# Routed attention and gated MLP on one core: four stages of three units a pair, one rotation of PSUM bank pairs, a bound moved to GpSimd

## The chip, the cores and the metric

The kernel runs on one core of a Trainium2 chip. The metric is the device time of one execution in microseconds (us). The engines are named as in the profile: PE is TensorE (its weight loads are listed as PEld), DVE is VectorE, ACT is ScalarE, POOL is GpSimd, SP is SyncE, which here only issues DMAs.

## The reference: what is computed

Four batches of eight heads, 768 tokens, head size 64. Every query and every key is assigned to the one of 16 centroids of its head that it is most similar to. A query attends only to the keys of its own cluster: softmax of `q k / 8` over these, times `v`. The result, read as 3072 tokens by 512, goes through an MLP:

```python
q_assign = argmax(normalize(q) @ normalize(c).T); k_assign = argmax(normalize(k) @ normalize(c).T)
scores = where(q_assign[:, None] == k_assign[None, :], q @ k.T / sqrt(64), -1e9)
attn = exp(scores - rowmax(scores)); attn /= attn.sum(-1) + 1e-9
x = attn @ v                              # then (B, S, H * D) as 3072 x 512
h = x @ w_in                              # 512 x 2048
out = (h * erf(softplus(h))) @ w_out      # 2048 x 512
```

All inputs and outputs are float32.

## The kernel before

**Work and units.** Heads are taken two at a time: a *pair* p (0 to 15), with head e=0 on partitions 0 to 63 and e=1 on 64 to 127. A pair's scores are computed transposed, in 12 *units*: two halves of 384 queries, and in each half six tiles j of 128 keys. One unit is a PSUM tile of 128 keys by 2 heads by 384 queries, which takes two PSUM banks. A core has eight banks. Two are the tiles `turned[0]` and `turned[1]`; the other six are the subject of this case.

**What a unit needs.** `products(u)` multiplies float32 k by q into the unit's two banks `sc`. `scores(u)` adds a bfloat16 matmul of `km` and `qm` on top: one-hot cluster vectors times a huge number, and one row that holds the query's shift (minus its maximum). `curve(u)` is ACT's exponential from PSUM into one of eight tiles `pr`. Later `accumulate(u)` adds `pr` on POOL (the softmax denominator; five additions per half, of which the first adds two tiles of `pr`), and `attend(u)` multiplies by v on PE into `turned[half]`. After the sixth unit of a half, `divide` sums the accumulated tile over partitions on PE into the other `turned` bank (the rows `turned<-more_out,minus`), takes Ln and Exp on ACT (`inv`), and in two further steps three DVE instructions (`den`, `turned`, `more_out`), then a DMA of the result to DRAM.

**Maxima, a pair ahead.** The shift of pair p+1 needs its row maxima. `maxima_step(p, i)`, 12 per pair, recomputes the masked scores in bfloat16 with queries on partitions (four matmuls into the two banks `wide`), and DVE reduces them from PSUM (`nmx`). After steps 5 and 11 a small DVE reduction (`lowest`) completes a half, and `turn` transposes the result on PE into `turned[half]`, from which ACT copies two rows into `qm`. The step runs six units ahead of the unit it stands beside. `masks` makes `qm` and `km` of pair p+1: a matmul with `pick` into a `turned` bank and an ACT copy out of it, four per pair. `similarities` and `choose` make the assignment of pair p+2 (one matmul group, four DVE instructions), `transposes` (two DVE instructions) and `vectors` (two ACT casts) its operands.

**Weight conversions.** In the background, weights are brought from DRAM as 512 KB pieces into five places and split into a form that later matmuls use: `size_and_rest` (two ACT instructions), `bounded` (DVE maximum with 2.0), `sign` (ACT), `shifted` (DVE shift by 3 bits), `summed` (POOL addition, which then frees the place and issues the next fetch on SP). 22 of the 32 pieces (`N_EARLY`) are done during the attention, two per pair. `FORMS` says in which periods the later pairs do sums of converted weights on DVE.

**The order of the work.** The order is written out by hand and kept: every engine executes its instructions in the order in which the program issues them, and waits where an operand or a buffer isn't ready. Before, a pair is six *periods* of two units (`period(p, i)`). A period issues, on PE: a `turn` if one is due (periods 0 and 3), a maxima step, the products of two units, a second maxima step, the scores of both, in period 3 the similarities, and then the `attend` of the two units of the period before, in periods 0 and 3 also the sum for `divide`. Masks stand in periods 0, 2 and 5. Tile mode matters on PE: products, scores, maxima and masks use 64 rows by 128 columns, so two matmuls (one per head) run side by side in the two row halves; `attend`, `turn` and the sum use 128 rows by 64 columns. In the profile these are marked `64*128` and `128*64`.

PSUM before: the maxima have their own two banks, `wide`, used by every step in turn; the units rotate through two pairs of banks (`ps_s`, two buffers).

After the attention comes the MLP, with the rest of the conversions; nothing in its order is touched.

## Time and profile before

| | us |
|---|---|
| median of three runs | 1022.67 (1022.65 to 1023.0) |
| the profiled execution's own time | 1022.77 |
| its span in the profile | 1021.1 |
| attention, steady: one pair (191.30 to 217.70) | 26.4 |
| first matmul of the MLP (`bank<-x_own,w_in`) | at 436.6 |

The span is what the trace covers, from the first to the last instruction; some 1.7 us of the execution lie around it. Busy times of PE overlap: a matmul's record runs until its result is out, while the next one has begun, so two consecutive *starts* tell more of PE's pace than durations do. In a row of the timeline the first number is the start, the second the time until the last of the merged instructions ends, and a bracket tells how long the engine was idle before and what released it. The granted clock was 1.00 in the whole attention.

### The profile page before, as it was taken

How to read it: one execution, taken by the hardware profiler on the slowest of the kernel's cores; microseconds unless marked ns; L12 is line 12 of the kernel's file. 1: busy time of each engine (PE TensorE's matmuls, PEld its weight loads, DVE VectorE, ACT ScalarE, POOL GpSimd, SP SyncE). 2: the span in 40 equal slices, each digit the busy share in tenths (PEclk: the TensorE clock that was granted, in tenths of full speed). 3: DMA queues.
4: the chain of work that ended last, by engine and by line, in shares of the span. 5: the costliest groups of instructions: out<-in, count | busy, mean ns of one | idle time of the engine just before them, and what ended most of it. 6: DMA issues, size and time to landing. Idle time of an engine off the chain costs nothing.

```text
span 1021.1 us, 15464 instructions
## 1 busy us (share of the span) xinstructions
PE 1013.9 (99%) x5930; PEld 726.1 (71%) x5930; DVE 695.8 (68%) x1305; ACT 515.0 (50%) x673; POOL 345.7 (34%) x229
## 2 busy tenths in 40 slices
PE   8999999999999999999999999999999999999998
PEld 3555555554555445478888888888888888888887
DVE  8777777777777777778875674756565547565754
ACT  3787877787777666567615142322233141505050
POOL 1777777777777667745130000000000000000000
PEclk9999999999999999999999999999999999999999
DMA  9344444444343311041100100110011000000001
GB/s 214 68 98 97 104 104 103 104 104 104 83 104 87 76 28 32 24 154 61 42 1 21 63 1 1 42 42 1 1 41 42 1 21 22 1 1 21 21 1 41
DMA packets 141641, 55.55 MB, mean 54 GB/s; under 512 B 127104, under 2 KB 131456, under 8 KB 141568
## 3 DMA queue, kind: packets, MB, share of 16 engines
q1 hardware_dynamic: 139216, 54.28, 20.8%
q8 instruction: 46, 0.75, 0.3%
q10 hardware_dynamic: 2352, 0.30, 0.2%
q14 instruction: 27, 0.22, 0.1%
HBM read 41.98 MB, written 12.58 MB: 53 GB/s over the span
## 4 chain that ended last, share of the span: by engine, by line
PE 97%; DVE 1%; POOL 0%; ACT 0%; issue 0%; DVEq 0%; ACTq 0%; POOLq 0%
PE bank L63 43%; PE turned L63 33%; PE sc L63 15%; PE wide L63 7%; DVE nmx L63 1%; POOL more_out L63 0%; DVE sims L63 0%; ACT inv L63 0%; DVE kT L63 0%; DVE qT L63 0%; ACT pr L63 0%; DVE hotT L63 0%; DVE wide L63 0%; DVE den L63 0%; DVE hot L63 0%
## 5 line engine op out<-in xcount | busy, mean ns | idle before, releaser
L63 POOL TENSOR_TENSOR more_out<-more_out,pr 128x768 f32<-128x768 f32 x128 | 223.5, 1746 | 67.6 <-ACT pr L63 62.5
L63 DVE TENSOR_REDUCE nmx<-wide 128x2 f32<-128x768 f32 x189 | 180.7, 956 | 95.1 <-PE wide L63 70.8
L63 ACT ACTIVATE pr<-sc 128x768 f32<-128x768 f32 x192 | 147.0, 810 | 75.0 <-PE sc L63 75.0
L63 PE MATMUL turned<-pr,in_v 128*64 128x386 f32 x768 | 145.5, 500 | 0.1
L63 DVE TENSOR_TENSOR g<-bank,g 128x256 f32<-128x256 f32 x222 | 89.5, 421 | 52.9 <-PE bank L63 46.3
L63 PE MATMUL bank<-x_own,w_in 128*128 128x256 f32 x424 | 104.5, 380 | 0.0
L63 PE MATMUL bank<-w_out,g 128*128 128x256 f32 x448 | 103.1, 379 | 0.0
L63 PE MATMUL sc<-qT,kT 64*128 64x384 f32 x528 | 99.7, 484 | 0.0
L63 PEld LDWEIGHTS turned<-pr,in_v 128*64 128x64 f32 x768 | 46.7, 136 | 72.2 <-issue 71.1
L63 PEld LDWEIGHTS bank<-w_out,g 128*128 128x128 f32 x448 | 85.2, 190 | 11.5
L63 PEld LDWEIGHTS bank<-x_own,w_in 128*128 128x128 f32 x424 | 80.4, 190 | 12.1 <-issue 1.2
L63 ACT COPY g<-bank 128x256 f32<-128x256 f32 x28 | 10.4, 372 | 152.5 <-PE bank L63 148.5
L63 DVE TENSOR_TENSOR osb<-bank,osb 128x256 f32<-128x256 f32 x87 | 35.4, 420 | 72.8 <-ACT osb L63 25.4
L63 ACT ACT_TABLE_LOAD x48 | 61.6, 1283 | 45.7 <-DVE g L63 45.0
L63 POOL TENSOR_TENSOR more_out<-pr,pr 128x768 f32<-128x768 f32 x32 | 58.8, 1837 | 58.5 <-ACT pr L63 58.5
L63 PE MATMUL bank<-x_more,more_in 128*128 128x256 f32 x296 | 76.0, 379 | 0.0
L63 PEld LDWEIGHTS <-qv 64*128 64x128 bf16 x384 | 25.6, 93 | 65.2 <-issue 51.1
L63 PE MATMUL wide<-kv,qv 64*128 64x384 bf16 x378 | 69.4, 328 | 1.1 <-ACT km L63 0.6
L63 PEld LDWEIGHTS sc<-qT,kT 64*128 64x128 f32 x528 | 56.6, 187 | 16.6 <-issue 1.2
L63 PE MATMUL wide<-km,qm 64*128 64x384 bf16 x378 | 68.3, 322 | 0.0
L63 PE MATMUL bank<-more_out,g_more 128*128 128x256 f32 x272 | 64.3, 379 | 0.0
L63 DVE TENSOR_TENSOR g<-a_s,g 128x512 f32<-128x512 f32 x96 | 62.4, 688 | 1.4 <-ACT a_s L63 1.4
(162 smaller groups left out, 1710.2 us busy)
## 6 DMA issues: line engine op xcount, KB each, us to landing
x_own<-in_moe_w_in_dram SPq DMA_DIRECT2D x13, 512.0 KB, 4.3
in_v<-in_v_dram SPq DMA_DIRECT2D x32, 192.0 KB, 2.9
x_dram<-more_out SPq DMA_DIRECT2D x32, 192.0 KB, 2.4
x_own<-x_dram SPq DMA_DIRECT2D x6, 1024.0 KB, 5.1
out_dram<-osb SPq DMA_DIRECT2D x23, 256.0 KB, 2.0
in_k<-in_k_dram SPq DMA_DIRECT2D x59, 96.0 KB, 2.7
in_q<-in_q_dram SPq DMA_DIRECT2D x58, 96.0 KB, 3.6
g_more<-in_moe_w_out_dram SPq DMA_DIRECT2D x6, 512.0 KB, 3.6
```

The lines of the kernel that those rows point to most:

```text
L63: ins = getattr(self.engine, name)(*args, **kw)
```

## The change

1. A pair is four *stages* of three units (`three(p, i)`) in place of six periods of two. A stage issues, per unit, one maxima step (`ahead`: seven units ahead in the steady state), the products, the scores and the exponential of that unit; then the `attend` of the three units of the stage before. `divide` begins at the end of stages 0 and 2, its DVE steps come in the next stage, all three between the second and the third maximum.
2. `wide` is gone. Maxima and units rotate through one pool of three pairs of banks (`two_banks`), in the order in which they are issued: maximum, unit, maximum, unit. So a tile takes the banks of the tile issued three places before it. `choose` takes its little maximum from the same rotation.
3. `turn` moves from the start of a period to the place between the second and the third unit's `attend`, in stages 1 and 3.
4. The masks stand at stage 0 (three of them) and stage 2 (one).
5. Three conversions in two pairs instead of four; all 22 are still done before the attention ends. `bounded` is issued on POOL for these, after the additions; `shifted` stands in stage 0 of each pair and in stage 2 of odd pairs, after the third maximum's reduction (and, in stage 0, ahead of the two `transposes`, which are now both there). `size_and_rest` is split in two.
6. `FORMS`, the places' order, the two `load_x` and the opening follow from that.

```diff
-    11: {5: 1}, 12: {0: 1, 2: 1, 5: 1}, 13: {0: 1, 2: 1, 5: 1}, 14: {0: 2, 2: 1, 3: 1, 5: 1},
-    15: {0: 1, 2: 1, 3: 2, 4: 2, 5: 2},
+    8: {2: 1}, 10: {2: 1}, 12: {0: 1, 2: 1}, 14: {0: 2, 2: 2, 3: 1}, 15: {0: 2, 1: 1, 2: 4, 3: 4},
...
-MASKS = {(0, 1): ("k", 0), (0, 2): ("k", 1), (2, 0): ("q", 0), (5, 0): ("q", 1)}
-FIRST_MASKS = {(2, 0): ("k", 0), (2, 1): ("q", 0), (2, 2): ("k", 1), (5, 0): ("q", 1)}
+MASKS = {(0, 0): ("k", 0), (0, 1): ("q", 0), (0, 2): ("k", 1), (2, 0): ("q", 1)}
+FIRST_MASKS = {(1, 1): ("k", 0), (1, 2): ("q", 0), (2, 0): ("k", 1), (2, 2): ("q", 1)}
...
-    ps_s = passing("ps_s", 2, space=PSUM)
-    wide = passing("ps_w", 1, space=PSUM).tile([P, 2, 512], F32, name="wide")
+    ps_s = passing("ps_s", 3, space=PSUM)
+
+    def two_banks():
+        return ps_s.tile([P, 2, 512], F32, name="sc", tag="s")
...
-    def bounded(n):
+    def bounded(n, engine=ve):
         w = w_steps[n][0]
-        ve.tensor_scalar(out=w, in0=w, scalar1=2.0, scalar2=None, op0=ALU.max)
+        engine.tensor_scalar(out=w, in0=w, scalar1=2.0, scalar2=None, op0=ALU.max)
...
-        mx = (wide[:, 0] if spare is None else spare)[:, 512 - n :]
+        mx = (two_banks()[:, 0] if spare is None else spare)[:, 512 - n :]
...
-    def maxima_step(p, i, sm=wide):
+    def maxima_step(p, i):
...
+        sm = two_banks()
...
-        sc = sc_of[u] = ps_s.tile([P, 2, 512], F32, name="sc", tag="s")
+        sc = sc_of[u] = two_banks()
...
-    def step_ahead(u):
-        p, i = divmod(u + NJ, 2 * NJ)
-        if p < NPAIR:
-            maxima_step(p, i)
+    ahead = [[u + NJ + 1] for u in range(len(units) - NJ - 1)] + [[] for _ in range(NJ + 1)]
+    ahead[0:NJ] = [[], [], [7, 8], [9], [10], [11]]
+    for u in range(NJ, 2 * NJ):
+        ahead[u] = [u + NJ]
+    ahead[2 * NJ - 1].append(3 * NJ)
...
+    def conversions(p, i):
+        a = 3 * (p // 2)
+        of = {
+            (0, 0): [(shifted, a - 1), (sign, a - 1)],
+            (0, 1): [(size, a)],
+            (0, 2): [(rest_of, a)],
+            (0, 3): [(size, a + 1)],
+            (1, 0): [(shifted, a), (sign, a)],
+            (1, 1): [(rest_of, a + 1)],
+            (1, 2): [(shifted, a + 1), (sign, a + 1), (size, a + 2)],
+            (1, 3): [(rest_of, a + 2)],
+        }[p % 2, i]
+        for f, n in of:
+            if 0 <= n < N_EARLY:
+                f(n)
+    def sums(p, i):
+        a = 3 * (p // 2)
+        of = {
+            (0, 1): [(summed, a - 1)], (0, 2): [(bounded, a)], (1, 0): [(bounded, a + 1)],
+            (1, 1): [(summed, a)], (1, 3): [(summed, a + 1), (bounded, a + 2)],
+        }.get((p % 2, i), [])
+        for f, n in of:
+            if 0 <= n < N_EARLY:
+                f(n, *([ge] if f is bounded else []))
+                if f is summed and n == N_EARLY - 4:
+                    load_x(0)
+                elif f is summed and n == N_EARLY - 1:
+                    load_x(1)
+    def three(p, i):
+        u = 2 * NJ * p + 3 * i
 
         def mask(place):
             which = (MASKS if p else FIRST_MASKS).get((i, place))
             if which:
-                return masks(p + 1, *which, turned[0 if i in (0, 5) else 1])
+                return masks(p + 1, *which, turned[0 if p and i == 0 else 1])
             return lambda: None
-        if u > 0:
-            for which in turns if i in (0, 3) else ():
-                turn(*which)
-                turns.remove(which)
-            step_ahead(u)
-        mask(0)()
-        next(part[0], None)
-        if u == 2:
-            next(routing[0])
-        products(u)
-        products(u + 1)
-        mask(1)()
-        if u > 0:
-            step_ahead(u + 1)
-        next(part[0], None)
-        scores(u)
-        scores(u + 1)
-        later = mask(2)
-        if i == 3:
+        for k in range(3):
+            for n in ahead[u + k]:
+                maxima_step(*divmod(n, 2 * NJ))
+            if k == 0:
+                mask(0)()
+            elif k == 1:
+                next(part[0], None)
+                next(part[0], None)
+            products(u + k)
+            if k:
+                copy = mask(k)
+            scores(u + k)
+            if k == 1:
+                copy()
+            curve(u + k)
+            if k == 2:
+                copy()
+        if u == 0:
+            similarities(1)
+            part[0] = choose(1)
+            next(part[0])
+            next(part[0])
+        elif i == 2:
             similarities(p + 2)
             routing[0] = choose(p + 2)
-        curve(u)
-        later()
-        curve(u + 1)
-        if u == 0:
-            step_ahead(1)
-            similarities(1)
-            routing[0] = choose(1, turned[0])
-            next(routing[0])
-            next(routing[0])
-            vectors(1, "q")
-            vectors(1, "k")
-        if i == 0 and early(n1 - 1):
-            shifted(n1 - 1)
-        elif i == 1 and early(n1):
-            size_and_rest(n1)
-        elif i == 2 and early(n1):
-            bounded(n1)
-            sign(n1)
+            for _ in range(3):
+                next(routing[0], None)
         elif i == 3:
-            if early(n1):
-                shifted(n1)
-            if early(n2):
-                size_and_rest(n2)
-        elif i == 4 and early(n2):
-            sign(n2)
-        elif i == 5 and early(n2):
-            bounded(n2)
+            run(routing[0])
+        conversions(p, i)
         for work in forms[: FORMS.get(p, {}).get(i, 0)]:
             work()
             forms.remove(work)
-        if i == 3:
-            for _ in range(3):
-                next(routing[0], None)
-        if i == 0:
-            if p:
-                transposes(p + 2, "q")
+        if u == 3 or p and i == 0:
+            transposes(p + 2)
+        if i == 2:
+            vectors(p + 2, "k")
+            vectors(p + 2, "q")
+        elif u == 0:
+            vectors(1, "q")
+            vectors(1, "k")
         elif i == 1:
             load(p + 1, "v", v, vp)
-            if p == 0:
-                run(routing[0])
-                transposes(2, "q")
-        elif i == 2:
-            transposes(p + 2, "k")
-        elif i == 4:
-            vectors(p + 2, "k")
-        elif i == 5:
-            run(routing[0])
-            vectors(p + 2, "q")
         if u > 0:
-            for w in (u - 2, u - 1):
+            for w in range(u - 3, u):
                 accumulate(w)
-            if i == 1 and early(n1 - 1):
-                summed(n1 - 1)
-            elif i == 4 and early(n1):
-                summed(n1)
-            for w in (u - 2, u - 1):
+            sums(p, i)
+            for w in range(u - 3, u):
                 attend(w)
-            if i % HJ == 0:
+                if w == u - 2:
+                    for which in turns:
+                        turn(*which)
+                    turns.clear()
+            if i % 2 == 0:
                 part[0] = divide(u - 1)
                 next(part[0])
-        mask(3)()
...
-    products(0)
-    warm(9, turned[0], zeros)
-    run(choose(0))
+    warm(11, turned[0], zeros)
+    place = two_banks()
+    run(choose(0, place[:, 1]))
...
-    step_ahead(0)
-    warm(2, turned[0], zeros)
+    products(0)
+    maxima_step(0, NJ)
+    products(1)
     turn(0, 0, (ae.copy, ve.tensor_copy))
...
-        for i in range(HJ * 2):
-            period(p, i)
-        if p == LAST_X:
-            load_x(0)
-            load_x(1)
-        if p == LAST_X + 2:
+        for i in range(4):
+            three(p, i)
+        if p == 13:
```

## The prediction

> **What bounds the kernel now.** I read the page's busy shares and chain first, then the windows of one pair, then the timelines of PE, DVE and POOL within a pair. The first fence has the page's rows and the window of one steady pair (its columns: length, then busy time and instructions of PE, PEld, DVE, ACT, POOL, granted clock, DMA).
>
> ```profile
> PE 1013.9 (99%) x5930; PEld 726.1 (71%) x5930; DVE 695.8 (68%) x1305; ACT 515.0 (50%) x673; POOL 345.7 (34%) x229
> PE 97%; DVE 1%; POOL 0%; ACT 0%; issue 0%; DVEq 0%; ACTq 0%; POOLq 0%
> 191.30:217.70 26.40, 26.38 (x202) 13.24 (x201) 19.85 (x31) 21.07 (x32) 19.67 (x13) 1.00 0.46 103
> ```
>
> In the attention PE sets the pace: 26.4 us a pair, while DVE, ACT and POOL have 5 to 7 us to spare. So a change pays if it shortens PE's own sequence, and costs if PE has to wait. The PE timeline of one period shows what the sequence is made of:
>
> ```profile
> 207.13 0.34 PE L63 MATMUL wide<-kv,qv 64*128 64x384 bf16 x2
> 207.30 0.33 PE L63 MATMUL wide<-km,qm 64*128 64x384 bf16 x2
> 207.46 1.45 PE L63 MATMUL sc<-qT,kT 64*128 64x384 f32 x8
> 208.75 0.33 PE L63 MATMUL wide<-kv,qv 64*128 64x384 bf16 x2
> 208.92 0.33 PE L63 MATMUL wide<-km,qm 64*128 64x384 bf16 x2
> 209.08 0.49 PE L63 MATMUL sc<-qm,km 64*128 64x384 bf16 x4
> 209.50 1.52 PE L63 MATMUL turned<-pr,in_v 128*64 128x386 f32 x8
> 210.95 0.34 PE L63 MATMUL wide<-kv,qv 64*128 64x384 bf16 x2
> ```
>
> By starts: a maxima step takes 0.33 us, the products of a unit 0.645, its scores 0.16. The row part lasts 207.13 to 209.50 = 2.37, of which 2 x 0.33 + 1.29 + 0.33 = 2.27 is work; `attend` of two units lasts 1.45, of which 1.30 is work (0.325 between starts, four times). A visit to the 128*64 mode thus costs 0.10 + 0.15, about 0.26.
>
> DVE, ACT and POOL: the reduction that frees `wide`, the copies of a `turn` and a scores matmul held by them, and what happens when DVE and POOL both want SBUF (columns as before).
>
> ```profile
> 207.67 0.96 DVE L63 TENSOR_REDUCE nmx<-wide 128x2 f32<-128x768 f32 x1 [1.02 <-PE wide L63]
> 216.27 0.97 ACT L63 CAST qm<-turned 1x384 bf16<-1x384 f32 x2
> 217.04 0.72 PE L63 MATMUL sc<-qm,km 64*128 64x384 bf16 x4
> 424.24 1.56 PE L63 MATMUL sc<-qT,kT 64*128 64x384 f32 x8
> 464.16 1.51 DVE L63 TENSOR_SCALAR w_out<-w_out 128x512 f32<-128x512 f32 x1
> 464.12 1.26 POOL L63 TENSOR_TENSOR more_out<-w_out,more_out 128x512 f32<-128x512 f32 x1
> 423.50 0.68 DVE L63 TENSOR_TENSOR more_in<-more_in,w_in 128x512 f32<-128x512 f32 x1
> 424.10 2.17 DVE L63 TENSOR_TENSOR w_in<-w_in 128x512 f32<-128x512 f32 x1
> 423.59 4.21 POOL L63 TENSOR_TENSOR more_out<-more_out,pr 128x768 f32<-128x768 f32 x2 [0.39 <-ACT pr L63]
> ```
>
> What to see: the scores at 217.04 take 0.72 instead of 0.49, since they wait for the copies. Products that PE had to wait for take 1.56, not 1.45: 0.105 of weight load shows. A DVE instruction on SBUF that meets a POOL addition already begun lasts until the addition ends (1.51 for a maximum that takes 0.42 alone; 2.17 for a sum that takes 0.68); if DVE is first (423.50, 0.09 ahead) it isn't held up.
>
> **The change, part by part, per pair.**
>
> *Removed.* Six visits to 128*64 become four: -0.51. Two waits of PE go: the scores behind the `turn` copies in period 3 (row part 2.61 instead of 2.37: 0.24), and in period 0 the second `km` mask behind the copy of the first (204.78 where its turn was at 204.6: 0.19): -0.43. Masks `k` and `q` use different row halves; side by side in stage 0 they cost one 0.16 and not two: -0.16. Together -1.10.
>
> *Waits added by the rotation.* Count from a stage's start, every engine in its order. Maximum 1 runs 0 to 0.33, its result is out at 0.50, its reduction runs 0.54 to 1.50. Unit 1: products 0.34 to 0.98, scores to 1.15; maximum 2 to 1.47. Unit 2 takes the banks of maximum 1, three places before: free at 1.50, its weight load starts 0.05 later (as after `lowest` in the rows, 423.59 to 423.65) and shows with 0.105, so its products are 0.19 late. Maximum 3 takes unit 1's banks; that exponential (0.81, from 1.41) ends at 2.22, before it is wanted at 2.47. Unit 3 takes maximum 2's banks: reduced by 2.63, wanted at 2.79, its weight load just hidden. So one wait of 0.19 in stages 1, 2 and 3; in stage 0 the masks spread the work and 0.08 is left: +0.65. Behind the waiting products stand the scores and all later PE work; nothing absorbs it.
>
> *`turn` and masks.* `turn` comes 1.35 after the attends begin, is out at 1.69, and the two copies (0.47 each) end at 2.69; the next stage begins at 2.27. Its first mask writes the same bank and wants it 0.34 into the stage; it gets it at 0.47: twice 0.13, and in stage 0 another 0.10, as the products' weight load is stuck behind the mask. +0.36. The scores that wait for the same copies come later, at 0.98: no second wait.
>
> *ACT.* In stage 2 of odd pairs a sign (1.36), a size (0.68) and both casts (0.89, 0.83) follow the third exponential; Ln and Exp of the sum start about 0.5 late, the next exponential too, and maximum 3 of stage 3 waits 0.18. Per pair +0.09.
>
> Sum so far: -1.10 + 1.10 = 0. The same count for the kernel before (six times 3.82, sums 1.29, turns 0.34, similarities 0.78, four masks 0.64, waits 0.43) gives 26.39, the measured pair.
>
> *`shifted` against POOL.* In stage 0 the shift follows the third reduction, which runs 3.20 to 4.16; it could start at 4.08. POOL's first addition of the half needs the second exponential, which ends at 3.90 (it stands behind the copy of mask `q`), and starts at 3.98, as additions do 0.08 after their exponential. POOL is 0.10 ahead, so the shift waits for its 1.81 and runs 5.79 to 6.21. Behind it are the two `transposes` (0.97 each), until 8.0; stage 0 is 6.89 long, so DVE comes free at 1.0 of stage 1, where the first reduction should start at 0.54. Unit 2 of stage 1 waits 0.66 instead of 0.19: +0.47 in pairs 1 to 13 (pair 0 has no shift there, 14 and 15 no transposes): +6.1. The bounds: 0, if the shift gets ahead; 1.0 per pair, if the shift in stage 2 of odd pairs (it can start at 6.6 behind `hot`, POOL's addition ends about 7.3 of 7.5) delays a reduction too. I take 0.47, from the worked order.
>
> The Trainium skill's page "SBUF — State Buffer" (Who interferes with whom) calls this an exclusive lock: the first has the shared ports for its whole instruction, the other is blocked. By it an addition that comes second would lose the shift's whole 0.42; the additions that met a shift in this trace took 1.86 instead of 1.68, so 0.18. POOL has room for either, the sum is the same.
>
> *`bounded` on POOL.* DVE loses 0.42 that was hidden in gaps: 0. On POOL the nearest rows are two-operand additions of 128x512 (1.29 to 1.37), the lower bound is DVE's 0.42; I take 1.3. Two pairs then need 20 additions (16 x 1.74 + 4 x 1.84), three `summed` (1.29) and three bounds: 43 of 53 us; the sum for `divide` is wanted more than 3 us after its last addition. Hidden: 0; if POOL's time went to 4.5 for one, it would fill up.
>
> The skill's "GPSIMD Engine Reference" (3. Performance versus the Vector engine) speaks against this move: elementwise work is about half as fast there. That makes an estimate of 0.83 for one bound and leaves the sum as it is. No row here shows the operation.
>
> *Opening, DMAs, end.* Before the first `turn` now stand products, a maxima step, products (1.6 us from 17.74; it began at 18.47): 0.9 later, of which what followed is already done: 0 to +0.9, I take +0.4. DMAs move with their steps; fetches have four places in hand, SP's loads a pair: 0. Pair 12 has a sum of weights in stage 0, which meets POOL as well: +0.5 (0 to 1). Pair 15 has no maxima after its first units and saves its visits, but four sums in stage 2 can last 2.17 each ahead of `den`, which the attends of stage 3 wait for: -0.5 (-1 to +1).
>
> Total: 0 + 6.1 + 0.4 + 0.5 - 0.5 = +6.5 on the profiled execution's own 1022.77 (0.1 above the median of the runs): **1029.3 us**. Over 15 pairs an error of 0.1 a pair is 1.5 us.
>
> **Rivals.**
> 1. *The shift wins the ports.* The lead is 0.10 us, out of a chain of ten steps. Then pairs stay at 26.4: 1022.8 + 0.4 - 0.5 = about 1023. For it: in the periods before, shifts met POOL idle or came 0.1 ahead. Against: the worked order.
> 2. *Faster: the rotation's wait isn't there.* If the first reduction's release reached PE before 1.36 (not 1.55) the weight load would be hidden, 0.65 a pair is won over 15.5 pairs, and with rival 1 the time is 1023 - 10 = 1013. For it: DVE is idle when maximum 1 ends. Against: 0.96 is the reduction's fixed length, and no row shows PE released sooner than 0.05 after.
> 3. *POOL becomes the bound.* Above 4.5 us for a bound, each further 1 us costs 1.5 a pair, 22 in all: beyond 1034. No row excludes it; the 1.3 speak against it.
>
> **How the numbers follow.** Forecast 58% (its own range 1026 to 1033: 0.25 a pair to either side), rival 1 20% (1020 to 1026), rival 2 17% (1012 to 1020), rival 3 or sums blocked in more stages 5%. A measurement of this kernel tells 0.2%, about 2 us, from no change. Slower by more: 0.58 + 0.05 + 0.01 = 0.64; within: 0.16 of rival 1; faster: 0.17 + 0.03 = 0.20. The range 1018.5 to 1034 leaves out most of rival 2 and rival 3.
>
> **What would show it.** Right: pairs of 26.8 to 27.0; PE weight loads for products released by `nmx` in each stage; the uint32 shift at some 2.1 us in stage 0; a first reduction of stage 1 that starts late behind `transposes`. Wrong: shifts of 0.42 throughout, pairs at or below 26.4, products never waiting for `nmx`, or POOL busy all the time.

## The result, and the profile after

The changed kernel takes 1041.18 us (median of five runs, 1039.59 to 1042.67) against 1022.81 before: 1.0176 times the time, 95% interval 1.0162 to 1.0191. The forecast was 1029.3 with a range to 1034. The direction was right, the size was not: 18 us more, not 6.5.

The profiled execution took 1039.63 with a span of 1037.9, 16.8 more than before's 1021.1. The next table cuts both traces at the first matmul of each pair's stage 0 (period 0 before) and at the first matmul of the MLP. The last column takes the prediction's terms apart by the same cuts.

| us | before | after | more | predicted |
|---|---|---|---|---|
| start to pair 1 | 43.82 | 48.87 | +5.05 | +0.4 |
| pairs 1 to 11 | 290.27 | 292.36 | +2.09 | +5.2 |
| pair 12 | 26.26 | 28.69 | +2.43 | +1.0 |
| pair 13 | 26.26 | 26.61 | +0.35 | +0.5 |
| pairs 14 and 15 | 50.01 | 56.93 | +6.92 | -0.5 |
| MLP to the end | 584.44 | 584.45 | 0 | 0 |

So the steady pairs lose less than forecast, and the two ends lose the time. The page of the changed kernel (busy times, the chain by engine), and behind it its waits of PE (us in total, times, longest):

```profile
PE 1016.0 (98%) x5930; PEld 710.2 (68%) x5930; DVE 722.3 (70%) x1283; ACT 526.2 (51%) x673; POOL 374.5 (36%) x251
PE 88%; DVE 9%; issue 1%; ACT 1%; DMA 1%; SPq 0%; DVEq 0%; ACTq 0%
```
```profile
PE sc L61 <- DVE nmx L61: 11.0, 16, 2.4
PE turned L61 <- DVE hotT L61: 1.5, 1, 1.5
PE turned L61 <- ACT qm L61: 1.3, 1, 1.3
```

DVE's share of the chain went from 1% to 9%, PE's from 97% to 88%. DVE isn't busy much longer (722 us instead of 696): it comes late in a few places. Before, the waits of PE for `nmx` were 0.4 us in total (waits under 0.15 are not listed).

**A steady pair.** The timelines of DVE, POOL and PE from the third reduction of stage 0 of pair 8 into stage 1:

```profile
238.79 1.82 POOL L61 TENSOR_TENSOR more_out<-pr,pr 128x768 f32<-128x768 f32 x1 [1.79 <-ACT pr L61]
238.89 2.00 DVE L61 TENSOR_SCALAR w_in<-w_in 128x512 uint32<-128x512 uint32 x1
240.81 0.96 DVE L61 STREAM_TRANSPOSE qT<-in_q 128x768 f32<-128x768 f32 x1
...
241.87 0.33 PE L61 MATMUL sc<-km,qm 64*128 64x384 bf16 x2
242.57 1.78 DVE L61 TENSOR_REDUCE nmx<-sc 128x2 f32<-128x768 f32 x2
243.54 0.92 PE L61 MATMUL sc<-more_out 64*128 64x384 f32 x4 [0.21 <-DVE nmx L61]
```

This is the predicted chain in the predicted place: POOL begins 0.10 ahead, the shift takes 2.00 instead of 0.42, the transposes end late, the first reduction of stage 1 starts at 242.57 although its matmuls (241.87 and 0.33 us long) were out at 242.20, and the products of the second unit wait. The pair takes 26.60. In one pair of this trace, pair 4, the race went the other way:

```profile
132.76 0.42 DVE L61 TENSOR_SCALAR w_in<-w_in 128x512 uint32<-128x512 uint32 x1
132.78 2.08 POOL L61 TENSOR_TENSOR more_out<-pr,pr 128x768 f32<-128x768 f32 x1 [1.93 <-ACT pr L61]
```

There DVE began 0.02 ahead, the shift took 0.42, the addition 2.08 instead of 1.82, and the pair took 26.31. So the collision costs 0.29 a pair, and a tenth of a microsecond decides it. The shift in stage 2 of odd pairs is held too, for 0.87, but into an idle stretch of DVE: odd and even pairs are alike.

**Pair 12** has a sum of weights behind that shift. The first products of stage 1 that need the reduction start at 352.04:

```profile
345.21 1.81 POOL L61 TENSOR_TENSOR more_out<-pr,pr 128x768 f32<-128x768 f32 x1 [1.80 <-ACT pr L61]
345.31 2.00 DVE L61 TENSOR_SCALAR w_out<-w_out 128x512 uint32<-128x512 uint32 x1
347.10 1.74 POOL L61 TENSOR_TENSOR more_out<-more_out,pr 128x768 f32<-128x768 f32 x1
347.22 2.17 DVE L61 TENSOR_TENSOR w_in<-w_in 128x512 f32<-128x512 f32 x1
...
352.04 0.92 PE L61 MATMUL sc<-qT,kT 64*128 64x384 f32 x4 [2.30 <-DVE nmx L61]
```

POOL's second addition starts 0.12 ahead of the sum. The shift ends 0.29 after the addition that held it, a sum 0.55 after, and by then POOL has begun the next one, 0.08 after the last. So each instruction in a row loses its own addition: the shift 1.6 and the sum 1.5. PE waits 2.30.

**Pair 15** shows what follows from a wait of that length (windows: length, busy time and count of PE, PEld, DVE, ACT, POOL, then the granted clock, DMA share and GB/s):

```profile
429.13 1.86 DVE L61 TENSOR_SCALAR w_out<-w_out 128x512 uint32<-128x512 uint32 x1
430.92 2.18 DVE L61 TENSOR_TENSOR more_in<-more_in,w_in 128x512 f32<-128x512 f32 x1
433.01 1.77 DVE L61 TENSOR_TENSOR w_in<-w_in 128x512 f32<-128x512 f32 x1
435.70 0.92 PE L61 MATMUL sc<-qT,kT 64*128 64x384 f32 x4 [2.37 <-DVE nmx L61]
```
```profile
434.00:436.00 2.00, 0.29 (x2) 0.30 (x4) 2.00 (x3) 0.00 (x0) 2.00 (x2) 1.00 0.38 60
436.00:438.00 2.00, 2.00 (x12) 0.86 (x9) 1.93 (x5) 0.81 (x1) 0.35 (x2) 0.63 0.93 326
438.00:440.00 2.00, 2.00 (x10) 0.74 (x8) 2.00 (x2) 0.81 (x1) 1.92 (x2) 0.52 0.66 243
```

After the wait the granted clock is at 0.63 and 0.52 for 4 us, which by estimate is another (1 - 0.63) x 2 + (1 - 0.52) x 2 = 1.7 us. The five runs of the changed kernel have mean clocks of 0.998 down to 0.995 and spans of 1037.9 to 1040.9; their median lies 1.5 above the profiled run, which would be about one more such stretch (the other runs left no trace).

**Pair 14** has two sums behind the shift of stage 0 as well (2.17 and 1.66; PE waits 2.29) and two more in stage 2, ahead of the first reduction of stage 3:

```profile
415.70 2.14 DVE L61 TENSOR_TENSOR w_in<-w_in 128x512 f32<-128x512 f32 x1
417.76 2.17 DVE L61 TENSOR_TENSOR more_in<-w_in,more_in 128x512 f32<-128x512 f32 x1
420.85 0.92 PE L61 MATMUL sc<-more_out 64*128 64x384 f32 x4 [0.77 <-DVE nmx L61]
```

**The opening**, PE's rows with the waits of pair 0, stages 1 and 2:

```profile
26.27 0.34 PE L61 MATMUL sc<-kv,qv 64*128 64x384 bf16 x2 [0.92 <-DVE nmx L61]
28.89 0.32 PE L61 MATMUL turned<-hotT,pick 64*128 64x384 bf16 x1 [1.48 <-DVE hotT L61]
38.47 0.85 PE L61 MATMUL turned<-more_out,ccT 128*32 128x384 f32 x8 [1.35 <-ACT qm L61]
```

The second maximum of stage 1 waits 0.92, the first mask 1.48 for the transposed choice (which stands on DVE behind that maximum's reduction), the similarities 1.35 for the copy of the last mask, which ACT makes after the third exponential. That is 3.75 of the 5.05; five smaller waits from 17.9 to 22.3 us come to 1.67, where before had four of 0.78 together.

### The profile page after: what moved, and what is told of

Same layout as the page of the kernel before. It is cut to its first block, busy times and chain, and to the rows that moved or that the text cites. A ratio compares the mean times of both kernels' runs of the same rounds, so it can differ in the third digit from the quotient of the medians.

```text
span 1037.9 us, 15476 instructions
## 1 busy us (share of the span) xinstructions
PE 1016.0 (98%) x5930; PEld 710.2 (68%) x5930; DVE 722.3 (70%) x1283; ACT 526.2 (51%) x673; POOL 374.5 (36%) x251
## 4 chain that ended last, share of the span: by engine, by line
PE 88%; DVE 9%; issue 1%; ACT 1%; DMA 1%; SPq 0%; DVEq 0%; ACTq 0%
PE bank L61 42%; PE turned L61 27%; PE sc L61 19%; DVE w_in L61 2%; DVE nmx L61 2%; DVE qT L61 1%; DVE more_in L61 1%; DVE kT L61 1%; DVE w_out L61 1%; DVE more_out L61 1%; ACT pr L61 0%; DMA in_k<-in_k_dram 0%; SPq L61 0%; DMA in_q<-in_q_dram 0%; ACT qm L61 0%
## 5 line engine op out<-in xcount | busy, mean ns | idle before, releaser
L61 POOL TENSOR_TENSOR more_out<-more_out,pr 128x768 f32<-128x768 f32 x128 | 218.8, 1709 | 41.0 <-ACT pr L61 33.9
L61 DVE TENSOR_REDUCE nmx<-sc 128x2 f32<-128x768 f32 x192 | 181.4, 953 | 66.2 <-PE sc L61 66.2
L61 ACT ACTIVATE pr<-sc 128x768 f32<-128x768 f32 x192 | 155.6, 811 | 72.7 <-PE sc L61 70.7
L61 PE MATMUL sc<-qT,kT 64*128 64x384 f32 x528 | 116.0, 506 | 6.8 <-DVE nmx L61 6.2
L61 PE MATMUL sc<-qm,km 64*128 64x384 bf16 x384 | 69.4, 324 | 0.8 <-ACT qm L61 0.6
L61 PE MATMUL sc<-kv,qv 64*128 64x384 bf16 x384 | 66.7, 327 | 1.3 <-DVE nmx L61 0.9
L61 PEld LDWEIGHTS <-qv 64*128 64x128 bf16 x384 | 23.1, 93 | 65.2 <-issue 62.8
L61 PE MATMUL sc<-km,qm 64*128 64x384 bf16 x384 | 65.8, 322 | 0.4 <-ACT km L61 0.4
L61 PEld LDWEIGHTS sc<-qT,kT 64*128 64x128 f32 x528 | 44.6, 186 | 29.9 <-DVE nmx L61 18.5
```

The source lines that it names most:

```text
L61: ins = getattr(self.engine, name)(*args, **kw)
```

## The experiments

The three candidates for the lost time are the blocked shift, the sums behind it and the opening; the rotation and the bound on POOL were to be priced by themselves. "Pairs" are lengths between the first matmuls of consecutive stages 0 (or periods 0), read from the traces. The kernel before, timed beside them, stayed at 1022.8 to 1022.95.

### The shift of stage 0 ahead of the third maximum

```diff
-            (0, 0): [(shifted, a - 1), (sign, a - 1)],
+            (0, 0): [(sign, a - 1)],
...
-            (1, 0): [(shifted, a), (sign, a)],
+            (1, 0): [(sign, a)],
...
         for k in range(3):
+            if (k, i) == (2, 0):
+                n = 3 * (p // 2) - 1 + p % 2
+                if 0 <= n < N_EARLY:
+                    shifted(n)
             for n in ahead[u + k]:
```

> The changed kernel, with one thing moved: the shift of stage 0 is issued before the third maximum's reduction, where POOL idles (1.79 us in the trace before its first addition), not after it. Theory (a DVE instruction on SBUF that comes 0.1 us after an addition of POOL has begun is held until that addition ends, and the sums behind it each meet the next addition): the shift takes 0.42 again, stage 1 gets back its 0.29 in ten of the pairs 1 to 11 (-3), pair 12 loses one addition less (-1.8), pairs 13 to 15 together -2 to -4: 1031 to 1034 us. Rival (the three-unit stages themselves cost the time, the blocked shift only fills idle DVE time): less than 1 us of gain, 1039 or more.

Measured: 1030.99 us (1.0081, interval 1.0066 to 1.0096), 10 less than the changed kernel. DVE and POOL in pair 8:

```profile
237.55 0.42 DVE L61 TENSOR_SCALAR w_in<-w_in 128x512 uint32<-128x512 uint32 x1
...
238.70 1.82 POOL L61 TENSOR_TENSOR more_out<-pr,pr 128x768 f32<-128x768 f32 x1 [1.83 <-ACT pr L61]
238.81 0.97 DVE L61 STREAM_TRANSPOSE qT<-in_q 128x768 f32<-128x768 f32 x1
```

The shift takes 0.42, while the transposition that now starts 0.11 after the addition isn't held. Pairs 1 to 11 take 26.31 or 26.32, all but one (26.41). Pair 12 falls from 28.69 to 26.87, pair 14 from 28.74 to 27.27, pair 15 from 28.19 to 25.11. So the theory holds, and one instruction of 0.42 us a pair had cost 10, together with the sums that it held up and the low clock of pair 15 (all of this trace from pair 1 on is at full clock). This trace began with a low clock of its own (0.77, 0.50, 0.50 and 0.53 in the four stretches of 1 us from 22), and its pair 1 starts at 50.44, 1.57 later than in the changed kernel, though nothing ahead of pair 1 differs.

### The sums one at a time

```diff
-    8: {2: 1}, 10: {2: 1}, 12: {0: 1, 2: 1}, 14: {0: 2, 2: 2, 3: 1}, 15: {0: 2, 1: 1, 2: 4, 3: 4},
+    8: {2: 1, 3: 1}, 9: {1: 1, 2: 1}, 10: {1: 1, 2: 1}, 11: {1: 1, 2: 1}, 12: {1: 1, 2: 1, 3: 1},
+    13: {1: 1, 2: 1, 3: 1}, 14: {1: 1, 2: 1}, 15: {3: 4},
```

> The changed kernel, with only the table of the sums changed: the 16 sums of weights stand one at a time in stages 1 to 3 of pairs 8 to 14, none in stage 0; the four of x stand last in pair 15. The shift stays where the change put it. Theory (several sums in a row on DVE lose one POOL addition each, and the reductions behind them come late): pairs 12, 14 and 15 give back 2.1, 2.5 and 2.5 to 4: 1031 to 1035 us, pair 12 at 26.6, and the steady pairs stay at 26.60. Rival (the end of the attention is long because the last stages have too little PE work to cover ACT and POOL, whatever the sums): under 2 us of gain, pair 15 stays at 28.

Measured: 1030.98 us (1.0082, interval 1.0067 to 1.0097). Pair 12 takes 26.59, pairs 14 and 15 take 25.83 and 24.11 instead of 28.74 and 28.19; the steady pairs stay at 26.60. One sum in a stage lasts 0.65 to 1.15 in most places and delays little (pairs 8 to 13 take 26.59 to 26.67):

```profile
353.79 1.05 DVE L62 TENSOR_TENSOR more_in<-w_in 128x512 f32<-128x512 f32 x1
355.35 0.96 DVE L62 TENSOR_REDUCE nmx<-sc 128x2 f32<-128x768 f32 x1 [0.51 <-PE sc L62]
```

After this sum, in pair 12, DVE still idles 0.51 until PE's next maximum. So the end of the attention wasn't long for want of PE work; the placement of the sums made it long. No low clock shows in this trace. Pair 15 at 24.11 is 0.53 shorter than before's 24.64: the saving that the prediction gave it is there once the sums are out of the way.

### The opening

```diff
-... (2, 0): ("k", 1), (2, 2): ("q", 1)}
+... (2, 0): ("k", 1), (2, 1): ("q", 1)}
...
             for n in ahead[u + k]:
                 maxima_step(*divmod(n, 2 * NJ))
+            if u == 0 and k == 2:
+                similarities(1)
+                run(choose(1, turned[0]))
...
-        if u == 0:
-            similarities(1)
-            part[0] = choose(1)
-            next(part[0])
-            next(part[0])
-        elif i == 2:
+        if i == 2:
```

> The changed kernel, with only pair 0 changed: the similarities and the whole choice of pair 1 stand before the products of the third unit, the little maximum is in a bank of its own again, and the last mask of the first pair is one unit earlier. Theory (the opening loses 0.92 at the second maximum of stage 1, 1.48 at the first mask, which waits for the transposed choice, and 1.35 at the similarities behind the last mask's copy): 3.75 less, 1035.5 to 1037 us, and pair 1 begins near 45.2 instead of 48.9. Rival (the time goes because the opening has no attends to put between the rows, so another wait takes the place of each): less than 1 us of gain.

Measured: 1038.03 us (1.0149, interval 1.0134 to 1.0164), pair 1 begins at 45.65: 3.22 earlier. Of the three waits none is left; one of 1.03 has come, for the products of the fifth unit, since the choice now stands ahead of a reduction on DVE. So the causes were right, and the gain was 3.2 and not 3.75. The end of the attention shows something else: pairs 12 and 14 take 30.36 and 30.38, where the changed kernel has 28.69 and 28.74.

```profile
348.85 1.65 PE L61 MATMUL sc<-qT,kT 64*128 64x384 f32 x4 [2.31 <-DVE nmx L61]
350.29 0.53 PE L61 MATMUL sc<-qm,km 64*128 64x384 bf16 x2
```

These are the same waits (2.31 here, 2.30 there), but this time the clock fell (0.71 and 0.50 in the two stretches of 2 us from 348): four products take 1.65 instead of 0.92, the scores 0.53 instead of 0.33. It costs 1.65 us each time. In pair 15 of this trace the wait is 2.36 and the clock stays at 1.00; the pair takes 26.55.

### The rotation alone, in the order before

```diff
-    ps_s = passing("ps_s", 2, space=PSUM)
-    wide = passing("ps_w", 1, space=PSUM).tile([P, 2, 512], F32, name="wide")
+    ps_s = passing("ps_s", 3, space=PSUM)
...
-    def maxima_step(p, i, sm=wide):
+    def maxima_step(p, i):
...
+        sm = two_banks()
```

> The kernel before, six periods of two units, with only the banks changed: maxima and units rotate through three pairs of banks. Theory (the rotation costs only where an order asks for a maximum's banks before its reduction of 0.96 has ended; here the second maximum asks 1.62 us after the first one's start and gets them at 1.55): 0 to +0.2 us a pair, 1022 to 1026 us. Rival (sharing the banks costs by itself, about 0.65 a pair wherever it is used): 1032 us.

Measured: 1022.94 us, a ratio of 1.000 (0.9991 to 1.001), pairs 26.39. The rotation costs nothing by itself. What costs is the order that asks for a maximum's banks sooner than its reduction can return them.

### The rotation's wait, taken away

```diff
-            out=nmx[:, :, t, half], in_=sm[:, :, 0:HW], axis=AX.X, op=ALU.max, negate=True
+            out=nmx[:, :, t, half], in_=sm[:, :, 0 : HW // 2], axis=AX.X, op=ALU.max, negate=True
```

The shift of stage 2 is moved ahead here as well.

> The changed kernel with both shifts ahead of the third maximum's reduction, and with reductions over half of the keys (192 of 384 columns, 0.55 us in place of 0.96), so the maxima leave out half of the scores. Theory (in each stage the products of the second unit wait for the first reduction, 0.19 in three stages and 0.08 in one, 0.65 a pair, and nothing else stands behind it): pairs fall from 26.3 to 25.65, and the whole time to about 10 us below that of the kernel with the shift moved alone. Rival (the products wait for something else, such as the exponential of the unit before): pairs stay above 26.1.

Measured: 1015.78 us. Pairs take 25.55 and 25.68 in turn, 25.62 on average, against 26.31 with whole reductions: 0.69, where the prediction's count of this wait was 0.65. By stages, the time from the first maximum to the first `attend` falls from 3.70 to 3.50 in stage 1, and in stage 2 the time to the similarities from 3.98 to 3.79. PE in stage 1 with nothing late, and the same place with whole reductions (pair 8 of the kernel with the shift moved alone):

```profile
196.51 0.33 PE L61 MATMUL sc<-km,qm 64*128 64x384 bf16 x2
196.68 0.81 PE L61 MATMUL sc<-qT,kT 64*128 64x384 f32 x4
...
242.91 0.33 PE L61 MATMUL sc<-km,qm 64*128 64x384 bf16 x2
243.16 0.92 PE L61 MATMUL sc<-more_out 64*128 64x384 f32 x4
```

The products follow the maximum by 0.17 and take 0.81. With the whole reduction they follow by 0.25 and take 0.92: 0.08 of the wait is a later start, and 0.105 is the weight load that shows. In odd pairs the third maximum of stage 3 starts 0.12 late; what holds it there wasn't followed.

### The bound on POOL alone, in the order before

```diff
-            bounded(n1)
             sign(n1)
...
-        elif i == 5 and early(n2):
-            bounded(n2)
...
             elif i == 4 and early(n1):
                 summed(n1)
+            elif i == 2 and early(n1):
+                bounded(n1, ge)
+            elif i == 5 and early(n2):
+                bounded(n2, ge)
```

> The kernel before, with only the lower bound of the early conversions moved to POOL, behind the additions of the same period. Theory (one bound takes 1.48 us on POOL, of which a pair has 6 us to spare, and DVE loses 0.42 that lay in gaps): 1022 to 1024 us, pairs stay at 26.39. Rival (POOL's additions come late behind the bounds, and with them the sum for the division): each bound delays the next addition by up to 1.5, 0.3 to 1 us a pair, 1027 to 1037 us.

Measured: 1025.71 us (1.0027, interval 1.0017 to 1.0037), pairs 1 to 11 at 26.6 instead of 26.39. That lies between the two expectations. The pairs make 2.4 us of it; the stretch behind the attention is 0.5 longer, which wasn't followed. POOL, DVE and PE in period 3 of pair 2:

```profile
82.10 1.48 POOL L63 TENSOR_SCALAR w_in<-w_in 128x512 f32<-128x512 f32 x1
83.55 3.45 POOL L63 TENSOR_TENSOR more_out<-more_out,pr 128x768 f32<-128x768 f32 x2
86.35 0.93 DVE L63 TENSOR_SCALAR w_in<-w_in 128x512 uint32<-128x512 uint32 x1
88.40 0.55 DVE L63 TENSOR_TENSOR hot<-sims,wide 128x384 bf16<-128x384 f32 x1
89.01 0.34 PE L63 MATMUL wide<-kv,qv 64*128 64x384 bf16 x2
```

The bound (1.48, up to 83.58) puts POOL's next two additions under the shift of the same pair, which takes 0.93 in place of 0.42. The choice behind it ends late, at 88.95; it reads its little maximum from `wide`, and the next maximum, due at 88.80 (0.74 behind the start of the sum for `divide`, 88.06), starts at 89.01. So the bound costs the pair nothing by its own 1.48 us, but it moves POOL's additions onto a DVE instruction.

### The same with the shift behind the choice

```diff
         elif i == 3:
-            if early(n1):
-                shifted(n1)
             if early(n2):
                 size_and_rest(n2)
...
         if i == 3:
             for _ in range(3):
                 next(routing[0], None)
+            if early(n1):
+                shifted(n1)
```

> The kernel before with the bounds on POOL (1025.7 us, pairs 26.59), and with the shift of the fourth period behind the first three steps of the choice on DVE, not ahead of them. Theory (the bound makes POOL's first addition start under that shift, the shift takes 1.2 us and not 0.42, the transposition of the similarities behind it comes late, and the sum for the division waits on PE for the bank that it reads): pairs 26.39 again, 1022.5 to 1023.5 us. Rival (the sum for the division waits for POOL's additions, which the bound delays): 1025.7 as it was.

Measured: 1024.70 us (1.0018, interval 1.0009 to 1.0027), pairs 26.53. Neither account fits. The wait after the sum for the division is gone (2.10 from the first `attend` to the next row instead of 2.30), but it had been the next maximum's, not the sum's, as the rows above show. The shift still meets an addition in its new place and takes 1.05:

```profile
88.57 1.05 DVE L63 TENSOR_SCALAR w_in<-w_in 128x512 uint32<-128x512 uint32 x1
89.54 0.94 DVE L63 TENSOR_REDUCE nmx<-wide 128x2 f32<-128x768 f32 x1
90.54 0.34 PE L63 MATMUL wide<-kv,qv 64*128 64x384 bf16 x2
```

Behind it the reduction is late, and the second maximum of the next period with it: 0.14 in place of 0.2. That the shift is held, and that this costs the time, holds for both; the wait that it ends in moved.

### The four repairs together

Both shifts ahead of the third maximum, the sums one at a time, the two edits of the opening.

```diff
+            if k == 2 and (i == 0 or i == 2 and p % 2):
+                n = 3 * (p // 2) + (p % 2 - 1 if i == 0 else 1)
+                if 0 <= n < N_EARLY:
+                    shifted(n)
```

> The changed kernel with four repairs together: both shifts ahead of the third maximum's reduction, the sums one at a time, the choice of pair 1 early with its own bank, the last mask of the first pair one unit earlier. Theory (these are all that makes it slower than before): pair 1 begins near 45.2, steady pairs take 26.3, pairs 12 to 15 about 26.3, 26.3, 25.5 and 24: 1021 to 1024 us. Rival (the gains overlap, or a new wait shows): 1028 or more.

Measured: 1023.62 us, ratio 1.0007 (0.9997 to 1.0016): as before the change. Pair 1 starts at 45.62, pairs 1 to 13 take 26.31 (one 26.42), pair 14 takes 25.59, pair 15 24.10. So the blocked shift, the sums and the opening account for the loss. Their gains overlap: apart they were 10.2, 10.2 and 3.2, together 17.6, since in pairs 12, 14 and 15 the shift and the sums behind it make one row of held instructions: either edit breaks it up, and either takes away the low clock of pair 15. What is left of the change is a pair 0.08 shorter, an end (pairs 14 and 15) 0.3 shorter and an opening 1.8 longer.

### Banks of their own for the maxima, in the new order

```diff
-    ps_s = passing("ps_s", 3, space=PSUM)
+    ps_s = passing("ps_s", 2, space=PSUM)
+    wide = passing("ps_w", 1, space=PSUM).tile([P, 2, 512], F32, name="wide")
...
-        sm = two_banks()
+        sm = wide
```

In the kernel with the four repairs.

> The changed kernel with the four repairs, but maxima in two banks of their own and units in two pairs of banks, as before the change. Theory (a maximum then waits for the reduction of the one before, 0.4 for the second and 0.24 for the third of a stage, less the 0.19 that the second unit waits with the rotation): 0.35 a stage more, pairs near 27.7, 1042 to 1047 us; so the rotation pays for itself in this order. Rival (the rotation gains nothing, only its own wait of 0.65 a pair comes and goes): pairs 25.7 to 26.3, 1014 to 1024.

Measured: 1065.2 us (1.0411, interval 1.0397 to 1.0425); pairs 28.34 against 26.31 with the rotation, so the rotation is worth 2.0 a pair in this order. The waits are at the expected places; by starts the second maximum is 0.41 late as counted, the third 0.42 and not 0.24 (PE's idle time in the brackets is shorter, since the record of the scores before still runs):

```profile
164.53 0.34 PE L62 MATMUL wide<-kv,qv 64*128 64x384 bf16 x2 [0.24 <-DVE nmx L62]
166.08 0.34 PE L62 MATMUL wide<-kv,qv 64*128 64x384 bf16 x2 [0.24 <-DVE nmx L62]
```

The total is beyond the expectation for two reasons: pairs are 0.6 longer than the 27.7 expected, some 9 us, and the opening, six maxima in a row on one pair of banks, ran with idle gaps and stretches of half clock, so that pair 1 starts at 56.23, 10.6 later than with the rotation.

### The bounds back on DVE

```diff
-            (0, 1): [(summed, a - 1)], (0, 2): [(bounded, a)], (1, 0): [(bounded, a + 1)],
-            (1, 1): [(summed, a)], (1, 3): [(summed, a + 1), (bounded, a + 2)],
+            (0, 1): [(summed, a - 1)], (1, 1): [(summed, a)], (1, 3): [(summed, a + 1)],
...
-            (1, 0): [(sign, a)],
+            (1, 0): [(bounded, a + 1), (sign, a)],
```

(and likewise at the two other places), in the kernel with the four repairs.

> The changed kernel with the four repairs (1023.6 us, steady pairs 26.31), and the lower bounds of the early conversions back on DVE, at the end of DVE's list of the same stages (in stage 0 ahead of the transposes). Theory (a bound on DVE is one more instruction that can meet an addition: in stage 0 of odd pairs it does, and the first reduction of stage 1 comes late; the other two find room): odd pairs 26.6, even ones 26.31, 1025 to 1026 us, so moving it to POOL is worth 2 us here. Rival (where the bound runs makes no difference, in gaps either way): 1023 to 1024.

Measured: 1027.62 us (1.0047, interval 1.0031 to 1.0062). Odd pairs take 26.60, even ones 26.31 (26.38 from pair 8 on), as expected. The bound of stage 0 has taken the shift's part:

```profile
102.50 2.01 DVE L62 TENSOR_SCALAR w_in<-w_in 128x512 f32<-128x512 f32 x1
106.19 1.78 DVE L62 TENSOR_REDUCE nmx<-sc 128x2 f32<-128x768 f32 x2
```

Pair 14 takes 27.54 instead of 25.59, which wasn't expected and adds 2. There a bound stands ahead of a sum, at the end of pair 13 and in stage 2 of pair 14, and the sum then meets the next addition:

```profile
389.56 0.54 DVE L62 TENSOR_SCALAR w_out<-w_out 128x512 f32<-128x512 f32 x1
390.02 2.16 DVE L62 TENSOR_TENSOR more_in<-more_in,w_in 128x512 f32<-128x512 f32 x1
```

Without the bound that sum takes 1.22. PE's products wait 1.37 behind this row and 0.49 behind the other.

In this order POOL is the better place, by 4.0 us, though the operation takes 1.49 there and 0.42 on DVE.

### Another order within the stage

The kernel with the four repairs; from pair 1 on a stage issues maximum, maximum, unit, unit, maximum, unit.

```diff
-            for n in ahead[u + k]:
+            if p and k == 2:
+                next(part[0], None)
+                next(part[0], None)
...
+            for n in ahead[u + k] if p == 0 or k == 2 else ahead[u] + ahead[u + 1] if k == 0 else []:
                 maxima_step(*divmod(n, 2 * NJ))
```

> The kernel with the four repairs, and from pair 1 on the order within a stage is maximum, maximum, unit, unit, maximum, unit in place of maximum, unit three times; the DVE steps of the division stand before the third maximum's reduction as before. Theory (the first mask then wants its bank after the copies of the turn have ended, and the second unit takes a place that was reduced or is free): the two waits for the turn and two of the four for a reduction go, steady pairs take 25.8, the whole 1012 to 1017 us, less than either kernel. Rival (the second maximum's reduction or the exponential holds the third maximum or unit instead): pairs at 26.3 or more, 1020 or more.

Measured: 1018.35 us, 0.9955 of the kernel before (0.994 to 0.9969): faster than both. Pairs take 25.90 (25.8 expected), 0.41 less than with the old order. PE at the start of stage 0:

```profile
201.08 0.34 PE L62 MATMUL sc<-kv,qv 64*128 64x384 bf16 x2
201.74 0.32 PE L62 MATMUL turned<-hotT,pick 64*128 64x384 bf16 x1
202.63 0.92 PE L62 MATMUL sc<-qT,kT 64*128 64x384 f32 x4
```

The mask stands 0.66 into the stage and waits for nothing; in the changed kernel it ran at 0.46, behind the copies. The second unit's products still show their weight load. The total missed the expected 1012 to 1017, since that took no account of the opening that is still 1.9 longer than before's.

A last kernel tried to win more there:

```diff
-    products(1)
     turn(0, 0, (ae.copy, ve.tensor_copy))
+    products(1)
...
-                run(choose(1, turned[0]))
+                part[0] = choose(1, turned[0])
+                next(part[0])
+                next(part[0])
...
-    13: {1: 1, 2: 1, 3: 1}, 14: {1: 1, 2: 1}, 15: {3: 4},
+    13: {1: 1, 2: 1, 3: 1}, 15: {3: 4},
```

(with the two sums of pair 14 placed in stage 3 of pairs 9 and 10, and one sum of pair 11 moved from stage 1 to stage 3)

> The kernel with the four repairs and the order maximum, maximum, unit, unit, maximum, unit (1018.35 us), with three small things more: in the opening the turn stands ahead of the second unit's products and the last two steps of the first choice behind the first reduction of the next stage; no sums in pair 14. Theory (waits of PE of 0.56 and 0.28 for the copies of the turn and 1.03 for that reduction become about 0.2 and 0.4, pair 14 falls from 26.3 to 25.9): 1016.3 to 1017.3 us. Rival (other waits take their place): 1018 or more.

Measured: 1018.71 us (0.996, interval 0.9948 to 0.9973), no better. The waits of the opening shrink, pair 1 starts at 45.17 instead of 45.70, but a new wait of 1.06 for a reduction has come at 41.66, and pairs 10 and 12 take 26.27 to 26.29 instead of 25.90. Pair 14, which the expectation had at 26.3, already took 25.51 and still does. The rival was right here.

## Why the prediction was wrong

**Right: what bounds the kernel, the ledger of a pair, and the collision.** The sum of removed visits and added waits was to leave a pair at 26.4 without the shift's collision; pair 4, the kernel with the shift moved and the one with the repairs have 26.31 to 26.32. The 0.09 between them is as much as was charged for a delay of ACT in odd pairs, and even and odd pairs are alike, so that delay isn't there. The single terms, but for the next two, were not measured one by one. The rotation's +0.65 measured 0.69. The mask's wait for the `turn` copies came to within a hundredth (0.47 into the stage forecast, 0.46 in the trace). The shift met POOL where the prediction said, in ten of eleven steady pairs, in nine of them by the lead that it said (0.09 or 0.10). Rival 1, the shift ahead of POOL, happened in pair 4; rival 2 is excluded by the reductions cut in half; rival 3 by the 1.49 of a bound and by POOL, which in the attention after the change is busy for 79% of the time and idles 2.2 us on average ahead of a half's first addition.

**Mis-sized: the collision's price in a steady pair**, 0.47 forecast and 0.29 measured. The held shift ended 0.28 after the addition, not its whole 0.42, and DVE was free 0.13 earlier. A row that the prediction shows had this already: the maximum at 464.16 ended at 465.67, 0.29 after the addition (465.38). Over eleven pairs, with the delay of ACT, this is 3 us less than forecast. The prediction also misread its trace where it weighed the opposite case: the additions of 1.86 each began 0.09 or 0.10 after a bound, not a shift, and no shift in that attention came ahead of an addition by less than 1.1. So the "0.1 ahead" in its support for rival 1 was that of bounds, which the change takes off DVE.

**Wrong: "Pair 12 has a sum of weights in stage 0, which meets POOL as well: +0.5".** The sum doesn't add its length to the shift's; it loses the next addition, 2.17 in place of 0.68, and what stands behind it is 2.3 late for PE. The trace before had it: the sum at 424.10, which the prediction showed, took 2.17, and the next one, at 426.19, 2.16. For pair 12 the prediction read this as the price of one meeting, when it is the price of each instruction in a row (for pair 15 it did allow 2.17 for each). Pair 12 lost 2.43 (with the shift moved, 0.6 of it remained).

**Wrong: "Pair 15 ... four sums in stage 2 can last 2.17 each ahead of `den`: -0.5 (-1 to +1)", and pair 14, for which nothing was counted.** The costly sums weren't those of stage 2 but the two in stage 0 of each, and the two in stage 2 of pair 14, in front of first reductions. The prediction excluded pair 14 because it has no transposes in stage 0; two sums of 2 us have the same effect. With the sums moved, pairs 14 and 15 give back 7.0, which includes the stretch of half clock. This is the largest part of the miss, and the kernel with the sums moved alone, 10 us faster, shows it.

**Wrong: "Opening ... I take +0.4".** The prediction looked at the work ahead of the first `turn` and at no wait behind it. It had the diff's new table for the first masks and the choice's place; followed with the same care as a steady pair, DVE's order would have shown the mask behind two reductions. Measured +5.05; 3.2 of it came back with three small edits.

**Not foreseen: the clock.** No row of the trace before shows a clock under 1.00, and the prediction priced a late reduction at its own length. In the changed kernel's trace one stretch of half clock adds some 1.7 us; the two in the kernel with the opening repaired add 1.65 each.

**`bounded` on POOL at 0.** The duration was 1.49 (1.3 taken), and no wait of PE in the changed kernel was traced to it. But the reason given, POOL has room, is not what decides: in the order before the same move costs 2.8 us, and in the new order moving it back costs 4.0. What decides is which DVE instruction POOL's additions then meet.

## What to carry to other kernels

Where two engines exclude each other on SBUF, an instruction's price is not its length but the length of what it meets, and each instruction of a row pays it again; so place such work one at a time, and where the other engine is idle by more than the uncertainty of the order (here over 1 us ahead of the half's first addition, where 0.1 us behind its start cost 10 us in all, with the sums that stood behind). Count the first and the last passes of a schedule as carefully as the steady one: here the steady pairs held two of the 17 us. And what rotating buffers cost is set by the order that asks for them: the same three pairs of banks cost nothing in one order and 0.7 us a pair in another.

## What was new about the hardware

**DVE against POOL on SBUF.** A shift that began 0.10 after an addition took 2.00 instead of 0.42 and ended 0.28 after it. The next addition starts 0.08 after the last, and the next DVE sum, 0.12 later, is held again, for 2.17. An addition that began 0.02 after a shift took 2.08 instead of 1.82, so POOL lost 0.26 where DVE loses 1.6. Reductions of 128x768 from PSUM (0.91 to 0.96) and the transpositions of 128x768 (0.93 to 0.98) weren't held in any of these traces, whether an addition ran or not. The Trainium skill's page "SBUF — State Buffer" (Who interferes with whom) says that whoever issues first has the shared ports for its whole instruction; the traces agree on which of the two is held, but an addition that came second lost 0.26, less than the 0.40 that was left of the shift. What cost the time here is that POOL begins its next addition 0.08 after the last, ahead of DVE's next instruction, which is then held in its turn.

**One-input work on POOL.** A maximum with a constant over 128x512 float32 took 1.49 on POOL and 0.42 on DVE, 3.5 times as long. The Trainium skill's "GPSIMD Engine Reference" (3. Performance versus the Vector engine), which the prediction drew on, has an elementwise addition of two inputs at 1.96 times DVE's time, about half its speed; for the maximum with a constant the measurement decides.

**The clock after a wait.** A wait of PE of 2.3 to 2.4 us was followed by about half the clock for 3 to 4 us in three places (436 us in the changed kernel, 348 and 406 in the one with the opening repaired), and not in three others of the same length (352 and 407 in the changed kernel, 2.30 and 2.29 us, and 436 in the one with the opening repaired, 2.36). In the kernel with the shift moved, such a stretch came at 22 us, behind five waits of 0.20 to 0.56 that the changed kernel has too, there at full clock. The length of the wait alone doesn't decide it. The Trainium skill's page "TensorE: Matmul & The Clock Gate" (What's actually happening) has the slow clock come after an idle window of about 3.4 us, longer than any of these waits, so here the measurement decides. It also says that the window runs freely and doesn't start with the kernel's work. If a window that is idle in part were enough, the place of a gap in it could account for the difference between equal waits, and for runs of one kernel that differ by 1.5 us. No run here shows the window itself, and the cause stays open.
